# Turns at the shared port, a longer lead for the x blocks' loads, and another place for one block of sums

## The chip, the cores and the metric

One core of one Trainium2 chip. TensorE (PE) multiplies; VectorE (DVE), ScalarE (ACT) and GpSimd (POOL) do the elementwise work; SyncE (SP) issues most of the DMAs. The metric is the device time of one execution in microseconds, the median of three runs. Smaller is better.

## The reference

A chunked attention with memory tokens feeds a mixture of eight experts, all of which are computed for every token and summed with weights that a Sinkhorn iteration makes from the gate's logits. The attention's output `x` has 3072 rows and 512 columns.

```python
# attention: chunks of 32 queries see 16 keys to the left, 8 to the right, and 8 memory keys
out[:, :, c_start:c_end] = softmax(scale * q_c @ k_full.T) @ v_full
x = attn_out.transpose(0, 2, 1, 3).reshape(3072, 512)
# experts
P = sinkhorn(exp(x @ w_gate), 8 rounds)
for e in range(8):
    h = np.maximum(x @ w1[e], 0.0)        # 512 -> 1024
    out += P[:, e:e+1] * (h @ w2[e])      # 1024 -> 512
```

## The kernel before

**Units.** The experts' work is cut into 48 units of 512 tokens: six units for each of eight experts, numbered n = 0 to 47. Each float32 operand is held as two float16 parts (high and rest), and each product is three passes. The matrix products are done as Strassen-like products of blocks, seven instead of eight, so that each operand also has sums and differences of blocks, which VectorE and GpSimd make. From n = 14 (`DEEP`) on the first product has a second level of such blocks (`inner`, L2511 on PE, L2545 on ACT, L2556 on DVE).

**A unit's steps.** `paired` makes two of the four hidden blocks at a time: PE products into the PSUM tiles px, py, pz (L2607); ACT reads the first of a tile (L2637), DVE adds the next to it (L2647), and the results stand in `c_all` or `cs_late`. One more block, the relu of the last product, is written by ACT (L2727) into a block of ring `r` (L2722) and read by DVE's sums (L2740), which go to `ss_all`. Then ACT casts to the high parts (L2761, L2770), and the rest is taken as a difference: by DVE for the plain blocks (L2779), and for the sums (L2797) by GpSimd for one block of each pair and by DVE for the other. `output` multiplies the hidden blocks with w2 (yx, yy, yz, L2448) while the next unit's `paired` runs, in an order that a string gives (`WOVEN`): f is a step of the first pair, b of the second, x and y are steps of the two output blocks of the unit before, t makes an x block (below), i and j are the steps of `inner`. The results are scaled into `acc` and added to DRAM by GpSimd's accumulating DMA (L3199).

**Other work in the stretch from 344 us to 800 us.** The x blocks that the second level needs are made in `inner_x`, by tokens in n = 6 to 17: where they can't be read in place, two loads (L2143) bring the parts of x into slots of ring `pre`, a part of the tile `p_all`; DVE adds them (L2182), GpSimd takes four differences (L2199), ACT and DVE split the result (L2206, L2210), and it is stored (L2221). `scaled` uses the same ring `pre`: it loads sums of the first expert (L2931), ACT scales them (L2940), and they are stored again (L2950). The next expert's weights are loaded (L1322), combined by GpSimd (L1370, L1038), split by ACT (L840) and DVE (L849) and stored (L999, L1355). The second level's weight blocks come back by L1250; those of the second pair lie in `p_all`, and the first of them, slot (1, 0), is where ring `r` has been. `hand_over` (for n = 14) gives the place over: the load waits on all who used the last block of `r`.

**The order of the work.** Each engine works off its list in order, and the lists are written by a planner (`Plan`) before the launch. It keeps a clock for each engine and a model of the DMA queue, picks the task that can start first (among several, the one that is due first; `due` works the due times back from PE's), and emits its instructions. From about 300 us on it holds one of {DVE, GpSimd} back while the other holds an operation marked `port` (two inputs in SBUF), by at least `held - LOCK`. Nothing in the program enforces that order between the two engines when they run: only data dependences do. For a consumer of a load it adds a guard of 1.0 us (`GUARDS`) to the landing that it expects.

Two places of the emitted program matter below; DVE and GpSimd in the order in which the planner emitted them:

```
near 540 us: DVE L2779, POOL L1038, DVE L2647, DVE L2779, POOL L2797, DVE L849, POOL L1038, ..., DVE L2797, DVE L2647
near 953 us: DVE L2797, POOL L2662, DVE L849 (256), POOL L1370, POOL L2797, DVE L2647, DVE L849 (512), DVE L2647
```

Of the kernel before, what the change touches and what calls it, by code (L numbers as in the profile page):

```python
# [51 lines left out]
GUARDS = {"ACT": 1.0, "DVE": 1.0, "POOL": 1.0, "SP": 1.2, "PE": 0.0}  # L52
YIELDS = 0.7
PRESSED = 1.0
AFTER = 300.0
# [6 lines left out]
PACED = 1  # L62
EARLIER = 20.0
BESIDES = 0.8


class Task:


    __slots__ = ("eng", "cost", "fn", "prio", "left", "ready", "end", "then", "takes", "frees", "n", "dma", "start", "size", "port", "also", "first", "lead", "tag")  # L70

    def engines(self):
        return (self.eng,) if self.also is None else (self.eng, self.also[0])
# [56 lines left out]
class Plan:  # L130
# [8 lines left out]
    def __init__(self):  # L139
        self.tasks = []  # L140
        self.free = {}
        self.fill = None
        self.pipe = 0.0
        self.counted, self.asks, self.fetches = 0, ASKS, []
        self.held = {"DVE": 0.0, "POOL": 0.0}
        self.drift = 0.0
        self.late = 1 << 30

    def add(self, eng, cost, fn, deps=(), prio=0.0, bufs=(), takes=None, frees=None, dma=0.0,
            size=0, port=None, since=0.0, also=None, first=False, lead=0.0, tag=None):  # L150
        t = Task()
        t.tag = tag
        t.eng, t.cost, t.fn, t.prio, t.takes, t.frees = eng, cost, fn, prio, takes, frees
        t.ready, t.end, t.then, t.n, t.dma = since, None, [], len(self.tasks), dma
        t.size, t.also, t.first, t.lead = size, also, first, lead
        t.port = eng == "POOL" if port is None else port
        if dma:
            t.cost = cost * ISSUE
        before = {id(d): d for d in deps if d is not None}
        for b in bufs:  # L160
            assert not b.closed
            before.update(
                {id(d): d for d in b.before if tag is None or d.tag is None or d.tag == tag}
            )
            b.users.append(t)
        t.left = len(before)
        for d in before.values():
            d.then.append(t)
        if frees is not None:
            frees.left += 1  # L170
        self.tasks.append(t)
        return t
# [90 lines left out]
    def due(self):  # L263

        when = {}
        for t in reversed(self.tasks[self.late :]):
            if t.eng == "PE":
                when[id(t)] = t.prio
                continue
            by = [when[id(s)] for s in t.then if id(s) in when]  # L270
            if not by:
                continue
            lag = LANDS + READY + QUEUES + t.dma if t.dma else LAG + 0.15
            late = t.lead + (BESIDES if t.eng == "POOL" else 0.0)
            when[id(t)] = min(by) - lag - late - t.cost * (1.0 + SHARED / 2 if t.port else 1.0)
            if t.frees is not None:
                when[id(t)] = min(when[id(t)], t.prio + 200.0 + HOLD)
            if t.eng in ("ACT", "DVE", "POOL", "SP"):
                t.prio = when[id(t)]

    def run(self):
        self.due()
# [9 lines left out]
        while left:  # L292
# [71 lines left out]
            else:  # L364
                clock[t.eng] = t.end = at + t.cost
                if self.fill is not None and t.eng in ("ACT", "DVE"):
                    clock[t.eng] -= OVERLAP
            t.fn()
            if t.frees is not None:
                b = t.frees  # L370
                b.left -= 1
                b.end = max(b.end, t.end + 0.15)
                if b.left == 0:
                    heappush(self.free[b.group], (b.end, b.bank))
# [3 lines left out]
            for s in t.then:  # L378
                s.left -= 1
                late = lag  # L380
# [5 lines left out]

                    late = MARGIN if s.prio - t.end > FAR else RISK if t.end > 10.0 else 0.0
                elif t.dma and sure:
                    late = GUARDS.get(s.eng, 0.0)
                s.ready = max(s.ready, t.end + late)  # L390
                if s.left == 0:
                    for e in s.engines():
# [5 lines left out]
def tile_chunked_attn_sinkhorn_moe(  # L398
# [123 lines left out]
    akeep = [dram.tile([P, DM], F32, name=f"akeep_{T}") for T in range(NT)]  # L522

    plan = Plan()
    add = plan.add
    plan.free["main"] = [(0.0, 2)]
    plan.free["early"] = [(0.0, 7)]
# [1601 lines left out]
    def inner_x(u, at, op, again, inside):  # L2129
# [46 lines left out]
        def part(i):  # L2176
# [7 lines left out]
            at,  # L2184
            [*xs, st],
            port=True,
        )
        last = [t]
        for i, a, b in (
# [398 lines left out]
    def paired(e, u, which, hs, place="h"):  # L2588
# [112 lines left out]
        else:  # L2701
# [17 lines left out]
            c12 = plus(pz, at(1), at(1), [t3, r6], [c], pz)  # L2719
            yield  # L2720
            t4 = run(px, P4, True, [c22])
            m = rings["r"].take(lambda _: shaped(home("p", 0, 2), [P, 2, GT]))  # L2722
            rest = lambda: m.t
            r = add(
                "ACT",
# [817 lines left out]
    def given(which, side):  # L3543
# [8 lines left out]

    WOVEN = {
        "plain": "tfffffxyfxyffftxybxybtxybxybtxybbxybbxy",
        "thirds": "ijijijijijijijFxyFxytFxyFFxyFxyBxyBtxyBxyBBxyxy",
        "deep": "ijijijijijijijFxyFxyFxyFFxyBxyBxyBxyBxyxy",
        "end": "ijijijijijijijFxByFxByFxByFFWBBxyxyxyxyxyxy",
# [20 lines left out]
    def weave(n, front, pair, tokens):  # L3578
# [10 lines left out]
        then = pair(1, "w1") if end else pair(1)  # L3589
        inside = [inner(e, u, p) for p in range(2)] if deep else [None] * 2  # L3590
        lists = {"f": front, "b": then, "F": front, "B": then, "x": back[0:1], "y": back[1:2], "i": inside[0:1], "j": inside[1:2]}
        kind = "end" if end else "plain" if not deep else "thirds" if e == FINE else "deep"
        for ch in WOVEN[kind]:
            if ch == "t":
                if tokens:
# [23 lines left out]
        if n == DEEP - 1:  # L3619
            for k in range(3):  # L3620
                rings["wid"].after((0, k), rings["xs"].last[0].users)
            rings["xs"].last[0].closed = True
            rings["m"].after(0, [t for k in (2, 3) for t in rings["stage"].last[k].users])
            old = xops[units[n - 1][1]][0].users
            for pos in range(3):
                rings["xf"].after(pos, old)
# [29 lines left out]
    for n, (e, u) in enumerate(units):  # L3656
# [75 lines left out]
        if n == NU:  # L3732
# [10 lines left out]
            rings["sd"].after(0, users["s", 0] + users["s", 1])  # L3743
            rings["r"].after(0, users["p", 0] + users["p", 1])
        if n == FINE * NU - 1:
            ring_ = rings["stage"]
            ring_.order = [i for i in ((ring_.n + j) % 4 for j in range(4)) if i < 2]
            ring_.n = 0
# [88 lines left out]
```

## Time and profile before

| | before |
|---|---|
| median of 3 runs | 1906.11 us (1903.03 to 1908.89) |
| the profiled execution, its own time | 1909.26 us |
| its span, first to last instruction | 1907.5 us |
| PE busy | 1865.1 us (98%) |
| DVE / ACT / POOL busy | 1525.2 / 1063.0 / 914.5 us |
| mean granted TensorE clock | 0.994 |

The profiled execution's time is its span and 1.8 us around it; it lies 3.2 us above the median of the runs. Differences are worked out on the profiled execution's own span and then taken from the median.

### The profile page before, as it was taken

The page shows a single profiled execution, that of the slowest core. Times are in us where ns is not written, and L with a number is a line of the kernel's source. Part 1 is how long each engine was busy: PE and PEld are TensorE (multiplying, and loading weights), DVE is VectorE, ACT ScalarE, POOL GpSimd, SP SyncE. Part 2 cuts the span into 40 slices and gives each one's busy share as a digit, 9 for nine tenths or more (in the row PEclk, how much of TensorE's full clock was granted, in tenths as well). Part 3 has the DMA queues.
Part 4 walks back from the last instruction along what each step waited for, and adds up shares of the span by engine and source line. Part 5 has one row for each costly group of instructions (what it writes and reads, how often), then busy time and mean ns, then how long its engine had stood idle before and what let it go on. Part 6 is the DMA issues. An engine that isn't in the chain of part 4 may idle for free.

```text
span 1907.5 us, 52507 instructions
## 1 busy us (share of the span) xinstructions
PE 1865.1 (98%) x21788; PEld 1624.9 (85%) x21788; DVE 1525.2 (80%) x2203; ACT 1063.0 (56%) x1804; POOL 914.5 (48%) x950
## 2 busy tenths in 40 slices
PE   9999999999999899999999999999999999999999
PEld 5677666787888898889989998998989998999998
DVE  5887778787888577787888888887988878887774
ACT  6665454665665455555655655655556555554453
POOL 3541221635785365644555355553665355553233
PEclk9999999999999999999999999999999999999999
DMA  9968843288779856987768965898678976786453
GB/s 218 222 141 210 210 128 132 98 277 208 242 209 281 230 144 169 278 264 212 184 193 265 285 173 167 248 278 219 160 206 259 297 165 183 237 237 188 123 128 95
DMA packets 336491, 389.27 MB, mean 204 GB/s; under 512 B 122300, under 2 KB 226492, under 8 KB 334652
## 3 DMA queue, kind: packets, MB, share of 16 engines
q1 hardware_dynamic: 312636, 342.92, 58.5%
q0 software_dynamic: 23616, 43.00, 15.2%
q8 instruction: 170, 2.79, 0.6%
q14 instruction: 69, 0.57, 0.1%
HBM read 253.18 MB, written 137.89 MB: 205 GB/s over the span
## 4 chain that ended last, share of the span: by engine, by line
PE 88%; DVE 3%; DMA 3%; ACT 2%; issue 2%; SPq 0%; POOL 0%; DVEq 0%; POOLq 0%; ACTq 0%
PE yx L2448 21%; PE px L2607 18%; PE yz L2448 11%; PE yy L2448 6%; PE yp L3333 5%; PE ix_1i L2511 4%; PE ix_0i L2511 4%; PE px L2448 2%; PE iz_1i L2511 2%; PE iz_0i L2511 2%; PE pz L2607 2%; PE pz L2448 1%; PE iy_1i L2511 1%; PE iy_0i L2511 1%; PE yp L3396 1%
## 5 line engine op out<-in xcount | busy, mean ns | idle before, releaser
L2448 PEld LDWEIGHTS <-h_all 128*128 128x128 f16 x4704 | 461.8, 98 | 55.3 <-DVE h_all L2779 0.2
L2607 PEld LDWEIGHTS <-w_all 128*128 128x128 f16 x3888 | 380.1, 98 | 63.4 <-issue 18.6
L2448 PE MATMUL yx<-w_all,h_all 128*128 128x256 f16 x2592 | 325.6, 273 | 0.0
L2607 PE MATMUL px<-x_whole,w_all 128*128 128x256 f16 x2544 | 313.6, 273 | 11.9 <-DVE cs_late L2647 9.9
L2448 PEld LDWEIGHTS <-h_late 128*128 128x128 f16 x2268 | 221.8, 98 | 27.4 <-DVE h_late L2797 1.7
L3199 POOL DMA_DIRECT2D akeep<-acc x164 | 147.4, 979 | 127.6 <-ACT acc L3139 54.3
L2797 POOL TENSOR_TENSOR h_all<-ss_all,h_all 128x1024 f16<-128x1024 f32 x56 | 126.1, 2251 | 145.8 <-ACT h_all L2770 126.9
L3029 ACT ACTIVATE acc<-yx,pscale 128x256 f32<-128x256 f32 x164 | 77.3, 472 | 193.0 <-PE yx L2448 185.2
L2448 PE MATMUL yx<-w_all,h_late 128*128 128x256 f16 x1248 | 163.7, 273 | 1.4 <-DVE h_late L2797 1.4
L2448 PE MATMUL yz<-w_all,h_all 128*128 128x256 f16 x1296 | 165.0, 273 | 0.0
L2647 DVE SCALAR_TENSOR_TENSOR cs_late<-px,stage_high 128x512 f32<-128x512 f32 x102 | 70.4, 690 | 87.7 <-PE px L2607 69.4
L2511 PEld LDWEIGHTS <-w_all 128*128 128x128 f16 x2376 | 136.9, 98 | 2.4 <-DMA w_all<-wkeep 1.6
L1038 POOL TENSOR_TENSOR w2f<-w2f 128x256 f32<-128x256 f32 x88 | 94.6, 1075 | 74.4 <-DVE wp L849 69.9
L2770 ACT CAST h_all<-ss_all 128x1024 f16<-128x1024 f32 x112 | 114.1, 1039 | 27.5 <-DVE ss_all L2740 27.5
L2545 ACT ACTIVATE stage_high<-ix_0i 128x512 f32<-128x512 f32 (+1 forms) x102 | 59.6, 585 | 101.3 <-PE ix_0i L2511 99.9
L1038 POOL TENSOR_TENSOR w1b<-w1b 128x256 f32<-128x256 f32 x88 | 94.2, 1071 | 38.2 <-DVE wp L849 27.1
L2797 POOL TENSOR_TENSOR h_late<-ss_all,h_late 128x1024 f16<-128x1024 f32 x27 | 59.7, 2211 | 91.6 <-ACT h_late L2770 86.5
L2607 PE MATMUL px<-x,w_all 128*128 128x256 f16 x768 | 95.4, 275 | 5.2 <-ACT cs_late L2637 4.4
L2448 PEld LDWEIGHTS <-w_all 128*128 128x128 f16 x924 | 89.2, 98 | 13.1 <-issue 1.4
L3333 PE MATMUL yp<-w_all,h_all 128*128 128x512 f16 x432 | 100.0, 379 | 0.0
L2647 DVE SCALAR_TENSOR_TENSOR c_all<-px,x_whole 128x512 f32<-128x512 f32 x102 | 70.1, 687 | 31.9 <-PE px L2607 31.0
L2662 POOL TENSOR_TENSOR stage_high<-stage_high 128x512 f32<-128x512 f32 x34 | 50.8, 1495 | 89.5 <-ACT stage_high L2545 68.3
(347 smaller groups left out, 4244.9 us busy)
## 6 DMA issues: line engine op xcount, KB each, us to landing
x_whole<-xkeep SPq DMA_DIRECT2D x203, 256.0 KB
akeep<-acc POOLq DMA_DIRECT2D x164, 256.0 KB, 5.6
wkeep<-wp SPq DMA_DIRECT2D x48, 512.0 KB
w_all<-wkeep SPq DMA_DIRECT2D x84, 256.0 KB
w_all<-wkeep SPq DMA_DIRECT2D x42, 512.0 KB
wkeep<-wp SPq DMA_DIRECT2D x48, 384.0 KB
wx_late<-ikeep SPq DMA_DIRECT2D x58, 256.0 KB
more<-ikeep SPq DMA_DIRECT2D x55, 256.0 KB
```

What stands on the lines that cost most here:

```text
L1038: lambda d=d, p=p, q=q, op=op: nc.gpsimd.tensor_tensor(d(), p(), q(), op=op),
L2448: nc.tensor.matmul(dst.t, a, b, start=(not more and n == 0), stop=(n == end), skip_group_check=more,)
L2511: nc.tensor.matmul(dst.t[:, k], left(k, op[0], wl), right(k, op[1], xl), start=(not more and n == 0 and k == 0), stop=(n == 2), skip_group ...
L2545: lambda: nc.scalar.activation(at(*to), src.t, AF.Copy, scale=DOWN),
L2607: nc.tensor.matmul(dst.t[:, f], ws[f][1](wl, kt), part(xl, kt), start=(not more and f == 0 and n == 0), stop=(n == 5), skip_group_check=True,)
L2647: lambda: nc.vector.scalar_tensor_tensor(to(), src.t, DOWN, other(), op0=ALU.mult, op1=ALU.add),
L2662: lambda: nc.gpsimd.tensor_tensor(part(2)(), part(2)(), part(1)(), op=ALU.add),
L2770: lambda f=f, h=h: nc.scalar.copy(h.t[:, 0, 3:7], s.t[:, f]),
L2797: lambda f=f, h=h, eng=nc.gpsimd if aside else nc.vector: eng.tensor_tensor(h.t[:, 1, 3:7], s.t[:, f], h.t[:, 0, 3:7], op=ALU.subtract),
L3029: lambda: nc.scalar.activation(acc.t[:, cols], src.t, AF.Copy, scale=f),
L3199: lambda a=a, dst=dst: nc.gpsimd.dma_start(dst, a.t, accum_op=ALU.add),
L3333: nc.tensor.matmul(py.t, hf.t[:, hl, where[fh], o : o + P], room(fp, WIDE * wl + DM * fh, WIDE * wl + DM * (fh + 1)), start=(fp == 0 and i ...
```

## The change

Four edits. (1) `turn`: from 300 us on, after a DVE task marked `port` is emitted, its last instruction is remembered; the next `port` task of GpSimd gets a wait on it. Each remembered instruction is used once: the first GpSimd operation after it waits, those that follow have only GpSimd's own order. GpSimd's DMA issues get no such wait, and nothing makes DVE wait on GpSimd. In the program before, the rule would give 262 GpSimd instructions a wait after 300 us. (2) `WARY`: where x parts are loaded for `inner_x`, the loads (L2143) are due 3 us earlier, and the planner lets the DVE add (L2182) start 3 us later after the landing that it expects. (3) The block of ring `r` that the second pair of n = 13 uses lies in `stage_high` in place of `p_all`; the load of slot (1, 0) then waits on the block of the first pair, and ring `m`, whose first block is `stage_high`, waits on the new one. (4) Unit n = 12 has an order of its own: the first pair's seven products all run ahead of the first x and y.

```diff
--- before.py
+++ after.py
@@ -62,12 +62,13 @@
 PACED = 1
 EARLIER = 20.0
 BESIDES = 0.8
+WARY = 3.0
 
 
 class Task:
 
 
-    __slots__ = ("eng", "cost", "fn", "prio", "left", "ready", "end", "then", "takes", "frees", "n", "dma", "start", "size", "port", "also", "first", "lead", "tag")
+    __slots__ = ("eng", "cost", "fn", "prio", "left", "ready", "end", "then", "takes", "frees", "n", "dma", "start", "size", "port", "also", "first", "lead", "tag", "wary")
 
     def engines(self):
         return (self.eng,) if self.also is None else (self.eng, self.also[0])
@@ -145,11 +146,12 @@
         self.held = {"DVE": 0.0, "POOL": 0.0}
         self.drift = 0.0
         self.late = 1 << 30
+        self.front = None
 
     def add(self, eng, cost, fn, deps=(), prio=0.0, bufs=(), takes=None, frees=None, dma=0.0,
-            size=0, port=None, since=0.0, also=None, first=False, lead=0.0, tag=None):
+            size=0, port=None, since=0.0, also=None, first=False, lead=0.0, tag=None, wary=0.0):
         t = Task()
-        t.tag = tag
+        t.tag, t.wary = tag, wary
         t.eng, t.cost, t.fn, t.prio, t.takes, t.frees = eng, cost, fn, prio, takes, frees
         t.ready, t.end, t.then, t.n, t.dma = since, None, [], len(self.tasks), dma
         t.size, t.also, t.first, t.lead = size, also, first, lead
@@ -267,7 +269,7 @@
             if t.eng == "PE":
                 when[id(t)] = t.prio
                 continue
-            by = [when[id(s)] for s in t.then if id(s) in when]
+            by = [when[id(s)] - (s.wary if t.dma else 0.0) for s in t.then if id(s) in when]
             if not by:
                 continue
             lag = LANDS + READY + QUEUES + t.dma if t.dma else LAG + 0.15
@@ -277,6 +279,21 @@
                 when[id(t)] = min(when[id(t)], t.prio + 200.0 + HOLD)
             if t.eng in ("ACT", "DVE", "POOL", "SP"):
                 t.prio = when[id(t)]
+
+    def turn(self, t):
+
+        eng = {"DVE": mybir.EngineType.DVE, "POOL": mybir.EngineType.Pool}[t.eng]
+        inst = next(i for i in reversed(self.tc.nc.cur_bb.bb.instructions) if i.engine == eng)
+        if t.eng == "DVE":
+            self.front = inst.name
+        elif self.front is not None:
+            self.tc.add_manual_dep(
+                inst,
+                self.front,
+                mybir.DependencyInfo(mybir.DependencyClass.Sync, mybir.DependencyReason.DATA),
+                reason="turns at the port",
+            )
+            self.front = None
 
     def run(self):
         self.due()
@@ -366,6 +383,8 @@
                 if self.fill is not None and t.eng in ("ACT", "DVE"):
                     clock[t.eng] -= OVERLAP
             t.fn()
+            if self.fill is None and at > AFTER and t.port and not t.dma:
+                self.turn(t)
             if t.frees is not None:
                 b = t.frees
                 b.left -= 1
@@ -386,7 +405,7 @@
 
                     late = MARGIN if s.prio - t.end > FAR else RISK if t.end > 10.0 else 0.0
                 elif t.dma and sure:
-                    late = GUARDS.get(s.eng, 0.0)
+                    late = GUARDS.get(s.eng, 0.0) + s.wary
                 s.ready = max(s.ready, t.end + late)
                 if s.left == 0:
                     for e in s.engines():
@@ -522,6 +541,7 @@
     akeep = [dram.tile([P, DM], F32, name=f"akeep_{T}") for T in range(NT)]
 
     plan = Plan()
+    plan.tc = tc
     add = plan.add
     plan.free["main"] = [(0.0, 2)]
     plan.free["early"] = [(0.0, 7)]
@@ -2184,6 +2204,7 @@
             at,
             [*xs, st],
             port=True,
+            wary=WARY if again else 0.0,
         )
         last = [t]
         for i, a, b in (
@@ -2719,7 +2740,10 @@
             c12 = plus(pz, at(1), at(1), [t3, r6], [c], pz)
             yield
             t4 = run(px, P4, True, [c22])
-            m = rings["r"].take(lambda _: shaped(home("p", 0, 2), [P, 2, GT]))
+            m = rings["r"].take(
+                lambda k: shaped(high[:, 0 : 2 * GT] if k else home("p", 0, 2), [P, 2, GT]),
+                int(which == 1 and (e, u) == units[DEEP - 1]),
+            )
             rest = lambda: m.t
             r = add(
                 "ACT",
@@ -3552,6 +3576,7 @@
 
     WOVEN = {
         "plain": "tfffffxyfxyffftxybxybtxybxybtxybbxybbxy",
+        "opens": "tfffffffxyfxyftxybxybtxybxybtxybbxybbxy",
         "thirds": "ijijijijijijijFxyFxytFxyFFxyFxyBxyBtxyBxyBBxyxy",
         "deep": "ijijijijijijijFxyFxyFxyFFxyBxyBxyBxyBxyxy",
         "end": "ijijijijijijijFxByFxByFxByFFWBBxyxyxyxyxyxy",
@@ -3589,7 +3614,7 @@
         then = pair(1, "w1") if end else pair(1)
         inside = [inner(e, u, p) for p in range(2)] if deep else [None] * 2
         lists = {"f": front, "b": then, "F": front, "B": then, "x": back[0:1], "y": back[1:2], "i": inside[0:1], "j": inside[1:2]}
-        kind = "end" if end else "plain" if not deep else "thirds" if e == FINE else "deep"
+        kind = "end" if end else "thirds" if deep and e == FINE else "deep" if deep else "opens" if n == FINE * NU else "plain"
         for ch in WOVEN[kind]:
             if ch == "t":
                 if tokens:
@@ -3620,7 +3645,8 @@
             for k in range(3):
                 rings["wid"].after((0, k), rings["xs"].last[0].users)
             rings["xs"].last[0].closed = True
-            rings["m"].after(0, [t for k in (2, 3) for t in rings["stage"].last[k].users])
+            rings["m"].after(0, rings["r"].last[1].users)
+            rings["r"].last[1].closed = True
             old = xops[units[n - 1][1]][0].users
             for pos in range(3):
                 rings["xf"].after(pos, old)
@@ -3743,6 +3769,7 @@
             rings["sd"].after(0, users["s", 0] + users["s", 1])
             rings["r"].after(0, users["p", 0] + users["p", 1])
         if n == FINE * NU - 1:
+            rings["r"].after(1, [t for k in (2, 3) for t in rings["stage"].last[k].users])
             ring_ = rings["stage"]
             ring_.order = [i for i in ((ring_.n + j) % 4 for j in range(4)) if i < 2]
             ring_.n = 0
```

## Rows read from the trace of the kernel before

**Rows 1.** The page's part 1: busy time and share of PE.
```profile
PE 1865.1 (98%) x21788; PEld 1624.9 (85%) x21788; DVE 1525.2 (80%) x2203; ACT 1063.0 (56%) x1804; POOL 914.5 (48%) x950
```
**Rows 2.** PE's waits: line, releaser, us in total, times, longest.
```profile
PE px L2607 <- DVE cs_late L2647: 10.6, 6, 2.4
PE iz_1i L2511 <- DMA p_all<-wikeep: 5.0, 1, 5.0
```
**Rows 3.** Busy time by stretch: PE, PEld, DVE, ACT, POOL, clock, DMA, GB/s.
```profile
640.00:660.00 20.00, 15.00 (x186) 14.19 (x185) 8.47 (x14) 8.59 (x15) 6.36 (x6) 0.91 0.81 170
```
**Rows 4.** PE's timeline, second level of n = 14 and of n = 16.
```profile
651.93 0.80 PE L2511 MATMUL iz_1i<-wx_late,p_all 128*128 128x128 f16 x6 [5.00 <-DMA p_all<-wikeep]
...
658.95 1.47 PE L2607 MATMUL px<-x_whole,w_all 128*128 128x256 f16 x12
...
725.13 0.50 PE L2511 MATMUL iz_1i<-wx_late,p_all 128*128 128x128 f16 x6
...
726.18 0.49 PE L2511 MATMUL ix_0i<-wx_late 128*128 128x128 f16 x6 [0.38 <-ACT stage_high L2545]
...
731.20 1.47 PE L2607 MATMUL px<-x_whole,w_all 128*128 128x256 f16 x12
```
**Rows 5.** Timelines of DVE, ACT and SP's queue around 645 us.
```profile
627.79 0.68 DVE L2740 SCALAR_TENSOR_TENSOR ss_all<-cs_late,p_all 128x512 f32<-128x512 f32 x1
...
643.51 1.29 DVE L2740 SCALAR_TENSOR_TENSOR ss_all<-c_all,p_all 128x512 f32<-128x512 f32 x2 [1.50 <-ACT p_all L2727]
...
648.74 0.49 ACT L2545 ACTIVATE x_whole<-ix_1i 128x384 f32<-128x384 f32 x1
...
644.87 0.34 SPq L1250 DMA_DIRECT2D p_all<-wikeep  x1
```
**Rows 6.** Timelines around 458 us: PE, ACT, DVE, SP's queue.
```profile
461.93 2.72 PE L2607 MATMUL px<-x,w_all 128*128 128x256 f16 x12 [4.41 <-ACT cs_late L2637]
...
460.15 0.51 ACT L2940 ACTIVATE p_all<-p_all,pscale 128x256 f32<-128x256 f32 x1 [5.93 <-DMA p_all<-akeep]
...
456.56 0.69 DVE L2182 TENSOR_TENSOR wx_late<-p_all 128x512 f32<-128x512 f16 x1 [4.47 <-DMA p_all<-xkeep]
...
450.08 0.47 SPq L2143 DMA_DIRECT2D p_all<-xkeep  x1
450.60 3.38 SPq L1322 DMA_DIRECT2D stage_high<-in_moe_w_dram  x4
...
454.67 6.00 SPq L2931 DMA_DIRECT2D p_all<-akeep  x3
```
**Rows 7.** Timelines of DVE, POOL and PE around 540 us.
```profile
536.45 0.94 DVE L2779 SCALAR_TENSOR_TENSOR h_all<-c_all,h_all 128x768 f16<-128x768 f32 x1
...
537.92 2.98 DVE L2779 SCALAR_TENSOR_TENSOR h_all<-c_all,h_all 128x768 f16<-128x768 f32 x1
...
536.54 3.50 POOL L2797 TENSOR_TENSOR h_all<-ss_all,h_all 128x1024 f16<-128x1024 f32 x1
...
544.08 1.47 PE L2607 MATMUL px<-x,w_all 128*128 128x256 f16 x12 [0.74 <-DVE cs_late L2647]
```
**Rows 8.** Timelines of DVE, POOL and PE around 955 us.
```profile
953.51 4.98 DVE L849 SCALAR_TENSOR_TENSOR wp<-w1b,sw,wp 128x512 f16<-128x512 f32 x1
...
953.90 1.55 POOL L2662 TENSOR_TENSOR stage_high<-stage_high 128x512 f32<-128x512 f32 x1
...
955.54 2.40 POOL L2797 TENSOR_TENSOR h_all<-ss_all,h_all 128x1024 f16<-128x1024 f32 x1
...
959.14 2.72 PE L2607 MATMUL px<-x_whole,w_all 128*128 128x256 f16 x12 [2.41 <-DVE cs_late L2647]
```
**Rows 9.** Timelines of POOL, DVE and PE in n = 12.
```profile
585.75 2.13 POOL L2797 TENSOR_TENSOR h_late<-ss_all,h_late 128x1024 f16<-128x1024 f32 x1 [5.14 <-DVE acc L3071]
...
589.50 1.22 DVE L2797 TENSOR_TENSOR h_late<-ss_all,h_late 128x1024 f16<-128x1024 f32 x1
...
590.77 0.94 PE L2448 MATMUL yx<-w_all,h_late 128*128 128x256 f16 x7 [1.45 <-DVE h_late L2797]
```

## The prediction, made before the result was known

> **What bounds the kernel now.** I read the page's part 1 first: TensorE is busy for 98% of the span [rows 1], so no other engine's busy time is worth anything in itself. All that a change in the order of work can give back are TensorE's holes, 1907.5 - 1865.1 = 42 us, and what a lower clock costs behind some of them. Edits 1 to 4 act only from about 300 us on (the planner's late part), so the holes of the attention stretch ahead of it stay.
>
> Second, the table of TensorE's waits says who ends the holes [rows 2], and the timelines say when. From 344 us on there are few long ones: 4.4 us at 457 [rows 6], 0.7 at 543 [rows 7], 1.45 at 589 [rows 9], 5.0 at 647 [rows 4], and four of 2.4 at 956, 1176, 1394 and 1610, which are one pattern, once for each of four experts [rows 8]; the group shows the first, and they are four of the six waits in the first row of the table [rows 2]. The rest are 1.4 us or less each. Third, for each hole, I read the timelines of the engine that ended it, to see what stood in front of the late instruction in that engine's list.
>
> The clock: in the stretch from 640 to 660 the granted clock is 0.91 [rows 3], so part of it ran at the lower level, 1.2 GHz instead of 2.4, behind the hole of 5.0. What that cost: from iz_1i to px there are the same products in n = 14 and in n = 16, 658.95 - 651.93 = 7.02 against 731.20 - 725.13 = 6.07, of which 0.38 is a hole [rows 4]. So 7.02 - 5.69 = 1.3 us are the clock's.
>
> **Edit 3, the place of one block of sums.** The hole of 5.0 ends with the landing of the load of slot (1, 0) [rows 4]. SP issued it at 644.87, just when VectorE's last two readers of ring `r`'s block, 643.51 to 644.80, were done [rows 5]; it landed 7 us later. With the block of the second pair in `stage_high`, the load waits on the readers of the first pair's block. These end at 628.5 [rows 5], so it can go 16 us earlier and is in place some 11 us before TensorE asks for it at 646.9. The cost of what is added: the relu is written and read as before, in another tile; the inner block's first write to `stage_high` now waits for the same two VectorE sums. It is wanted when TensorE comes back to that tile, 0.67 us after iz_1i's start in n = 16 [rows 4], at 647.6; a write takes 0.49 [rows 5] and the sums end at 644.80, so over 2 us of cover are left by the inner level's first four products; if the sums came later by more than that, their lateness would appear in the hole of ix_0i.
>
> What is late next: ScalarE writes x_whole<-ix_1i only at 648.74 to 649.23 [rows 5], behind casts for h_all that were put ahead of it. Without the DMA's hole, TensorE comes to the product that needs it about 1.2 us after iz_1i's start (as 725.13 to 726.18 less 0.38, and the next product of 0.5 [rows 4]), so at about 648.1. If ScalarE keeps that order, a hole of 1.2 opens; if the planner, which no longer expects a late load, puts the short read first, there is none. The nearest row is the same place in n = 16, 0.38 [rows 4]; I take 0.4, with 0 to 1.2 as bounds. Edit 3: 5.0 + 1.3 - 0.4 = 5.9 us (5.1 to 6.3).
>
> **Edit 1, turns at the port.** Near 540 us GpSimd's L2797 starts at 536.54, VectorE's second L2779 at 537.92, and this takes 2.98 where the one ahead of it took 0.94 [rows 7]. In the emitted order that L2779 stands directly ahead of GpSimd's L2797, so the turn falls on the right instruction: GpSimd would start behind it. VectorE gains up to 2 us, and TensorE's hole of 0.74, which ended with a VectorE instruction queued behind, goes. I take 0.7; bounds 0 and 0.74. What GpSimd then does later is its L2797 by some 2 us, and behind it two differences and DMA issues for data of the next expert; its h block is used after the plain blocks' products, so nothing on TensorE waits on it here.
>
> At 955 us it is otherwise. VectorE's L849 takes 4.98 while GpSimd runs L2662, L1370 and L2797 without a break [rows 8]; this holds up c12 and makes the hole of 2.4. But in the emitted order GpSimd's L1370 and L2797 stand ahead of this L849. Their turns are taken by the VectorE instructions before it, long over: GpSimd is behind the plan here, and the edit has no wait in the other direction. So I count nothing for these four holes; the other bound, that all go, is 4 x 2.4 = 9.6 us and the clock's part, 2.72 - 1.47 = 1.25 for this one [rows 7, 8], say 12 in all.
>
> One rule speaks against edit 1. The trace first: VectorE's L849 started at 953.51 and was not through when L2662 ended at 955.45, but only after L2797, 957.94 [rows 8]: it was passed over between two GpSimd instructions. The Trainium skill ("SBUF — State Buffer", Who interferes with whom) calls the port pair an exclusive lock, held for one instruction by whichever engine issues first. By that rule the turn only moves the same block from VectorE to GpSimd, edit 1 would be worth 0 and the sum below 6.6; by the trace, which disagrees in that a late VectorE instruction pays for several GpSimd instructions, it is worth 0.7.
>
> **Edit 4, the order in n = 12.** The hole of 1.45 at 589 ends with VectorE's L2797 at 589.50 [rows 9]. In the new string that product still has the same seven f, two b and the earlier x and y in front of it, so TensorE comes to it no later; what can change is the lists of VectorE and ScalarE, since the first pair's sums are ready earlier. Bounds 0 and 1.45; I take half, 0.7. No instruction is added.
>
> **Edit 2, the lead.** VectorE's add L2182 waits 4.47 us at 452 to 456.5 for its load [rows 6]; the edit puts other work in front of it. But the hole at 457 doesn't come from there. It ends with ScalarE's L2637, which is queued behind L2940; and that waits 5.93 for a load of `scaled`, issued by SP at 454.67, behind four weight loads of 3.38 [rows 6]. That load gets no lead. Its bounds: if the new order of SP's queue happens to put it in front of the weight loads, 4.4 + 1.3 of clock = 5.7 us go; if the led x loads take its place in the queue instead, it is later by one issue, 0.47 [rows 6], and the hole grows by that. I count 0, the nearer row.
>
> **The sum.** 5.9 + 0.7 + 0.7 + 0 = 7.3 us off the span of 1907.5, to 1900.2. The profiled execution's own time, 1909.26, is 3.2 above the median; I take the difference from the median: 1906.1 - 7.3 = 1898.8 us. This kernel's measurement tells a difference of some 0.3%, 5.7 us, from none; the forecast is just beyond.
>
> **Rivals.**
> - *SP's new order clears the hole at 457 too.* For: edit 2 moves the due times in that queue, at that place. Against: not of the load that is late. 7.3 + 5.7 = 13.0: 1893.1 us.
> - *The four starved L849 are cured as well*, because the new plan puts them ahead of GpSimd's run. For: the planner's list is remade. Against: the pattern came out the same for four experts with different starts. 7.3 + 12 = 19.3: 1886.8 us.
> - *The load's hole is replaced.* ScalarE's order stays (hole 1.2), the clock still falls behind it or the sums come late into `stage_high`, and edits 1 and 4 move nothing: 5.0 - 1.2 = 3.8, and 1.3 of clock kept: 1902.3 us, no change that can be told.
> - *A new hole like that of 457 elsewhere*, since all loads between 344 and 640 are ordered anew while the DMA queue is full: 7.3 - 5.7 = 1.6: 1904.5 us.
> - *Slower: the turn holds GpSimd's h block.* In n = 7 to 12 GpSimd's L2797 can be close to its use: 585.75 to 587.88, with TensorE at that product at 589 [rows 9]. Were it given its turn behind VectorE's L2797, 589.50 to 590.72, it would end at 592.9: a hole of some 3.9 and 1.3 of clock, 5.2 us. Three such units of the six cost 15.6 against 7.3: 1914.4 us; it decides from the third. Against: in the present list it stands ahead of that instruction.
>
> **Chances.** Forecast 0.48, with its own range 1894 to 1902; first rival 0.17; second 0.07; third 0.11; fourth 0.09; slower 0.08. Faster by over 0.3% means under 1900.4: three quarters of the forecast's 0.48, and the first two rivals, 0.60. Slower: the last rival and a little of the fourth, 0.10. Within: 0.30. Leaving out the second and the last rival (0.15), the range runs from 1888 to 1908.
>
> **What the profile after would show.** Edit 3: p_all<-wikeep issued well before 640, no wait of iz_1i on a DMA, at most 1.2 us on ScalarE's x_whole, clock 1.00 from 640 to 660. Edit 1: VectorE's L2779 near 540 back at 0.95, GpSimd's L2797 behind it; at 955, 1176, 1394 and 1610 L849 still at about 5 us and the hole still 2.4. Edit 2: L2182 no longer waiting, the ScalarE wait at 457 still there. The prediction is wrong if those four holes are gone, if ScalarE's wait on L2931 is gone, or if TensorE waits on h_all or h_late at places where it did not.

## The result, and the profile after

The changed kernel takes 1878.36 us (median; 1877.90 to 1879.52) beside 1904.57 (1902.98 to 1908.89) for the kernel before in the same job: a ratio of 0.986, 95% interval 0.9841 to 0.9878. The gain is 0.014 x 1904.6 = 26.7 us where 7.3 were forecast, and the time lies below the range. The profiled execution has a span of 1877.5 us against 1907.5, 30.0 less.

In the changed kernel's file the lines stand about 20 lower down: L849 is L869, L1038 L1058, L1370 L1390, L2607 L2628, L2637 L2658, L2647 L2668, L2779 L2803, L2797 L2821, L2931 L2955, L2940 L2964. Kernels of the experiments differ from that by up to 2.

Part 1 of the page of the changed kernel, which answers to [rows 1]:

```profile
PE 1855.1 (99%) x21788; PEld 1619.5 (86%) x21788; DVE 1486.8 (79%) x2203; ACT 1064.1 (57%) x1804; POOL 865.4 (46%) x950
```

TensorE's idle time went from 42.4 us to 1877.5 - 1855.1 = 22.4. The other 10.0 us are busy time with the same 21788 matmuls: the mean granted clock rose from 0.994 to 1.000, and 0.6% of 1865 is 11. So two thirds of these 30.0 us are holes and one third is the clock. Not all of the clock is the edits' work: before, the granted clock was 0.83 from 20 to 40 us, ahead of anything that they touch, beside 460 to 480 (0.83), 640 to 660 (0.91), 940 to 980 (0.97 and 0.94) and 1600 to 1620 (0.91), which stand behind holes that went.

But for n = 12, TensorE's matmuls come in the same order in both kernels, so one and the same matmul can be looked up in both profiled executions. By its start, the changed kernel is 1.0 us ahead at 343 us, before any edit shows. It gains 7.2 us across the hole at 457, 0.9 across that at 543, 1.6 at 589, 6.7 at 647, and 4.0, 2.5, 2.5 and 4.1 at the four of [rows 8]: 29.5 in all; what is gained and lost elsewhere comes to half a us.

VectorE and GpSimd lost 38.4 and 49.1 us of busy time with the same instruction counts; more on that at the end.

The table of TensorE's waits in the changed kernel, for [rows 2] (line, releaser, us in total, times, longest):

```profile
PE ix_1i L2532 <- ACT x_whole L2566: 3.3, 5, 1.4
...
PE px L2628 <- DVE c_all L2668: 1.0, 1, 1.0
...
PE px L2628 <- DVE cs_late L2668: 0.8, 1, 0.8
```

The row of 10.6 us for VectorE's cs_late is down to 0.8, the 5.0 us on the DMA are gone, and there is no row left for ScalarE's cs_late, which made the hole at 457. Now the places, in timelines of the changed kernel. The second level of n = 14, for [rows 4, 5], and then the window that answers to [rows 3]:

```profile
637.10 0.50 PE L2532 MATMUL iz_1i<-wx_late,p_all 128*128 128x128 f16 x6
...
642.62 1.47 PE L2628 MATMUL px<-x_whole,w_all 128*128 128x256 f16 x12
...
619.42 0.32 SPq L1270 DMA_DIRECT2D p_all<-wikeep  x1
...
633.80 1.29 DVE L2764 SCALAR_TENSOR_TENSOR ss_all<-c_all,stage_high 128x512 f32<-128x512 f32 x2 [1.45 <-ACT stage_high L2751]
...
636.34 0.49 ACT L2566 ACTIVATE stage_high<-ix_0i 128x384 f32<-128x384 f32 x1
636.79 0.49 ACT L2566 ACTIVATE x_whole<-ix_1i 128x384 f32<-128x384 f32 x1
```

```profile
640.00:660.00 20.00, 20.00 (x210) 18.20 (x208) 17.31 (x29) 11.36 (x20) 9.73 (x12) 1.00 0.59 177
```

The load is issued 17.7 us before TensorE's use of it, where it was 7.1. VectorE's sums are through with `stage_high` at 635.1 and the inner block's first write there starts at 636.34. From iz_1i to px it is 5.52 us, where it was 7.02, and the clock is 1.00.

Around 458 us, for [rows 6], SP's queue and ScalarE:

```profile
447.37 0.47 SPq L2163 DMA_DIRECT2D p_all<-xkeep  x1
447.89 2.25 SPq L1342 DMA_DIRECT2D stage_high<-in_moe_w_dram  x4
450.24 0.52 SPq L2974 DMA_DIRECT2D akeep<-p_all  x1
450.86 0.43 SPq L2955 DMA_DIRECT2D p_all<-akeep  x1
...
455.37 0.51 ACT L2964 ACTIVATE p_all<-p_all,pscale 128x256 f32<-128x256 f32 x1 [1.07 <-DMA p_all<-akeep]
```

The whole train of x load, four weight loads and load of `scaled` runs some 3 us earlier: the x load at 447.37 (before 450.08), the late load at 450.86 (454.67). ScalarE waits 1.07 for it instead of 5.93, and TensorE not at all.

At the first of the four starved L849, three more lines of the kernel before beside [rows 8], and then VectorE and GpSimd in the changed kernel:

```profile
953.48 0.75 POOL L1370 TENSOR_TENSOR ws_halves<-w1b,w1b 128x128 f32<-128x128 f32 x1
...
955.12 0.73 POOL L1370 TENSOR_TENSOR ws_halves<-w1b,ws_halves 128x128 f32<-128x128 f32 x1
...
959.02 0.73 DVE L849 SCALAR_TENSOR_TENSOR ws_halves<-ws_halves,sw 128x512 f16<-128x512 f32 x1
```

```profile
937.83 2.51 DVE L869 SCALAR_TENSOR_TENSOR wp<-w1b,sw,wp 128x512 f16<-128x512 f32 x1
940.26 0.68 DVE L2668 SCALAR_TENSOR_TENSOR cs_late<-px,stage_high 128x512 f32<-128x512 f32 x1
941.73 1.84 DVE L869 SCALAR_TENSOR_TENSOR ws_halves<-ws_halves,sw 128x512 f16<-128x512 f32 x1 [0.79 <-ACT ws_halves L860]
...
936.10 0.55 POOL L1390 TENSOR_TENSOR ws_halves<-w1b 128x128 f32<-128x128 f32 x1 [9.30 <-DMA wikeep<-ws_halves]
...
937.80 0.75 POOL L1390 TENSOR_TENSOR ws_halves<-w1b,w1b 128x128 f32<-128x128 f32 x1
938.22 1.56 POOL L2683 TENSOR_TENSOR stage_high<-stage_high 128x512 f32<-128x512 f32 x1
940.48 0.46 POOL L1390 TENSOR_TENSOR ws_halves<-w1b,ws_halves 128x128 f32<-128x128 f32 x1 [0.70 <-DVE wp L869]
940.89 2.13 POOL L2821 TENSOR_TENSOR h_all<-ss_all,h_all 128x1024 f16<-128x1024 f32 x1
```

The bracket at 940.48 is the turn: the last of the four L1390 waits on L869. In both kernels the third of them starts 0.03 us ahead of VectorE's instruction, and L2683 (L2662 before) after it. Before, the fourth and L2797 followed without a break, and L849 ended 0.55 us behind L2797; now L869 ends 0.56 behind L2683. It takes 2.51 instead of 4.98, and c12, the VectorE instruction behind it, comes in time. The next L869 takes 1.84 where it took 0.73, with L2821 beside it, and TensorE doesn't wait for that. GpSimd's h block ends 5.2 us after L869's start where it ended 4.4 after it, and nothing waits for it.

### The profile page after: what moved, and what is told of

It reads as the page before. It is cut to its first block, busy times and chain, and to the rows that moved or that the text cites. A ratio compares the mean times of both kernels' runs of the same rounds, so it can differ in the third digit from the quotient of the medians.

```text
span 1877.5 us, 52657 instructions
## 1 busy us (share of the span) xinstructions
PE 1855.1 (99%) x21788; PEld 1619.5 (86%) x21788; DVE 1486.8 (79%) x2203; ACT 1064.1 (57%) x1804; POOL 865.4 (46%) x950
## 4 chain that ended last, share of the span: by engine, by line
PE 92%; DMA 3%; DVE 2%; ACT 1%; issue 1%; SPq 1%; POOL 0%; DVEq 0%; POOLq 0%; ACTq 0%
PE yx L2469 23%; PE px L2628 19%; PE yz L2469 11%; PE yy L2469 6%; PE yp L3357 5%; PE ix_1i L2532 4%; PE ix_0i L2532 4%; PE px L2469 2%; PE pz L2628 2%; PE iz_0i L2532 2%; PE iz_1i L2532 2%; PE pz L2469 1%; PE iy_0i L2532 1%; PE iy_1i L2532 1%; PE yp L3420 1%; PE py L2628 1%
## 5 line engine op out<-in xcount | busy, mean ns | idle before, releaser
L2628 PEld LDWEIGHTS <-w_all 128*128 128x128 f16 x3888 | 379.0, 98 | 46.2 <-issue 2.3
L2628 PE MATMUL px<-x_whole,w_all 128*128 128x256 f16 x2544 | 312.4, 273 | 1.8 <-DVE c_all L2668 1.0
L2821 POOL TENSOR_TENSOR h_all<-ss_all,h_all 128x1024 f16<-128x1024 f32 x56 | 122.8, 2192 | 124.5 <-ACT h_all L2794 49.3
L2668 DVE SCALAR_TENSOR_TENSOR cs_late<-px,stage_high 128x512 f32<-128x512 f32 x102 | 70.4, 690 | 91.4 <-PE px L2628 70.4
L1058 POOL TENSOR_TENSOR w2f<-w2f 128x256 f32<-128x256 f32 x88 | 77.8, 884 | 83.8 <-DVE wp L869 32.5
L1058 POOL TENSOR_TENSOR w1b<-w1b 128x256 f32<-128x256 f32 x88 | 79.9, 909 | 48.8 <-issue 9.4
L2821 POOL TENSOR_TENSOR h_late<-ss_all,h_late 128x1024 f16<-128x1024 f32 x27 | 57.6, 2134 | 81.2 <-ACT h_late L2794 45.3
L2628 PE MATMUL px<-x,w_all 128*128 128x256 f16 x768 | 94.1, 273 | 0.0
L2668 DVE SCALAR_TENSOR_TENSOR c_all<-px,x_whole 128x512 f32<-128x512 f32 x102 | 70.2, 688 | 24.3 <-PE px L2628 22.9
L2821 DVE TENSOR_TENSOR h_all<-ss_all,h_all 128x1024 f16<-128x1024 f32 x56 | 81.8, 1460 | 5.6 <-ACT h_all L2794 5.6
```

Of the source, the lines that this page charges most:

```text
L1058: lambda d=d, p=p, q=q, op=op: nc.gpsimd.tensor_tensor(d(), p(), q(), op=op),
L2628: nc.tensor.matmul(dst.t[:, f], ws[f][1](wl, kt), part(xl, kt), start=(not more and f == 0 and n == 0), stop=(n == 5), skip_group_check=True,)
L2668: lambda: nc.vector.scalar_tensor_tensor(to(), src.t, DOWN, other(), op0=ALU.mult, op1=ALU.add),
L2821: lambda f=f, h=h, eng=nc.gpsimd if aside else nc.vector: eng.tensor_tensor(h.t[:, 1, 3:7], s.t[:, f], h.t[:, 0, 3:7], op=ALU.subtract),
```

## The experiments

The ratios are to the kernel before on the same chip; 1% is 19 us.

| kernel | ratio | 95% interval |
|---|---|---|
| edit 1 alone | 0.9934 | 0.9910 to 0.9958 |
| edit 2 alone | 0.9960 | 0.9943 to 0.9977 |
| edit 3 alone | 0.9981 | 0.9964 to 0.9998 |
| edit 4 alone | 0.9994 | 0.9978 to 1.0010 |
| all but edit 1 | 0.9950 | 0.9933 to 0.9968 |
| all but edit 2 | 0.9901 | 0.9873 to 0.9930 |
| all but edit 3 | 0.9906 | 0.9876 to 0.9936 |
| all but edit 4 | 0.9874 | 0.9842 to 0.9906 |
| edit 1, waits behind L849 only | 0.9919 | 0.9904 to 0.9934 |
| edit 1, all other waits | 0.9971 | 0.9949 to 0.9993 |
| edit 2, earlier due only | 0.9942 | 0.9925 to 0.9958 |
| edit 2, later add only | 0.9997 | 0.9978 to 1.0016 |
| all edits, waits behind L849 only | 0.9861 | 0.9836 to 0.9886 |
| all edits, again | 0.9858 | 0.9832 to 0.9884 |

One kernel "without" an edit is the changed kernel with that edit undone as the diff shows; "alone" has the other three undone.

**Edit 1, the turns.** Undone by

```diff
-            if self.fill is None and at > AFTER and t.port and not t.dma:
-                self.turn(t)
```

Alone:

> Edit 1 alone on the kernel before. Theory T (the turn itself cures the four starved L849, because in the planner's order GpSimd's fourth L1370 comes behind L849, not ahead of it): the four holes of 2.4 us near 956, 1176, 1394 and 1610 and what the clock costs behind two of them go, and the 0.7 near 543: some 12 to 14 us less than before, L849 (512 columns) near 954 at about 2.5 us in place of 4.98. The holes of 4.4 at 457 and 5.0 at 647 stay. Rival P (the four went because edits 2 to 4 made the planner's list anew, as on record in the prediction): 0.7 us less at most, L849 still at 4.98.

All but it:

> The changed kernel without edit 1. If the turn alone cures the four starved L849: the four holes of 2.4 come back with the clock behind some of them, 1878 + 10 to 13 = 1888 to 1891 us. If the remade list had a part in it, less comes back.

Alone 0.66%, 12.6 us; taken out of the whole, 0.90%. TensorE's waits with edit 1 alone, and with all but edit 1:

```profile
PE iz_1i L2532 <- DMA p_all<-wikeep: 5.3, 1, 5.3
PE px L2628 <- ACT cs_late L2658: 4.8, 2, 4.6
```

```profile
PE px L2626 <- DVE cs_late L2666: 12.3, 7, 2.4
```

With the turns alone, the holes at 457 and 647 stay and VectorE's cs_late is off the head of the table; without them it leads the table, and the holes of 457 and 647 are gone. The plan of "edit 1 alone" is that of the kernel before, instruction for instruction, so no remade list did this: the wait did. With it the four starved L869 (512 columns) take 2.50 to 2.51 us, where they took 4.98 to 4.99.

The hole of 0.7 near 543 is gone too, but not by the turn behind L2779 (here L2803) that the prediction names. GpSimd there, with edit 1 alone:

```profile
541.60 0.72 POOL L1058 TENSOR_TENSOR stage_high<-stage_high 128x256 f32<-128x256 f32 x1 [1.24 <-DVE h_all L2821]
542.30 2.11 POOL L2821 TENSOR_TENSOR h_all<-ss_all,h_all 128x1024 f16<-128x1024 f32 x1
```

In the planner's order GpSimd's h block stands behind an L1058 whose turn falls on VectorE's own h block.

Then the waits themselves were divided, in the plan of the kernel before. A flag marks the VectorE tasks that `split` adds (L849), and the wait is given only behind those, or (`not self.half`) only behind the others:

```diff
-            self.front = inst.name
+            self.front, self.half = inst.name, t.half
...
-            self.tc.add_manual_dep(
+            if self.half:
+                self.tc.add_manual_dep(
```

Only behind L849:

> Edit 1 alone, and of its waits only those that stand behind VectorE's L849 (101 of 384 in the planner's order); the plan is that of the kernel before. Theory: the four holes of 2.4 us near 956, 1176, 1394 and 1610 hang on one such wait for each expert, L1370 behind L849; all four go, the small hole near 543, which hangs on a turn behind L2779, stays; ratio 0.994 to 0.996, nearly all of the 0.9934 that edit 1 gave alone. Rival: the gain is spread over many waits; then about a quarter of it, 0.998, is here.

Only behind the others:

> Edit 1 alone, and of its waits all but those behind VectorE's L849 (283 of 384); the plan is that of the kernel before. Theory: the four holes of 2.4 us stay, the one near 543 goes; ratio 0.998 to 1.0. Rival, the gain is spread: three quarters of it are here, 0.995.

GpSimd with the waits behind L849 only; then VectorE, GpSimd and TensorE with the others only:

```profile
949.97 1.55 POOL L2685 TENSOR_TENSOR stage_high<-stage_high 128x512 f32<-128x512 f32 x1
952.22 0.46 POOL L1392 TENSOR_TENSOR ws_halves<-w1b,ws_halves 128x128 f32<-128x128 f32 x1 [0.70 <-DVE wp L870]
```

```profile
954.38 4.98 DVE L870 SCALAR_TENSOR_TENSOR wp<-w1b,sw,wp 128x512 f16<-128x512 f32 x1
...
954.77 1.55 POOL L2685 TENSOR_TENSOR stage_high<-stage_high 128x512 f32<-128x512 f32 x1
955.99 0.73 POOL L1392 TENSOR_TENSOR ws_halves<-w1b,ws_halves 128x128 f32<-128x128 f32 x1
956.40 2.39 POOL L2823 TENSOR_TENSOR h_all<-ss_all,h_all 128x1024 f16<-128x1024 f32 x1
...
960.01 1.47 PE L2630 MATMUL px<-x_whole,w_all 128*128 128x256 f16 x12 [2.41 <-DVE cs_late L2670]
```

The quarter of the waits that stands behind L849 (101 of 384) carries all of edit 1 (0.81%, the whole 0.66%, intervals overlapping). That of these only one for each expert matters was not tried. The small hole near 543 was expected to stay and is down to 0.2. With the others the first place is as it was before, 4.98 and 2.41; in that profile three of the four holes are there, and the hole of 0.7 near 543 is gone. Their 0.29% lies between the two expectations, so what they are worth in the kernel before stays open between 1 and 10 us. In the changed kernel it was tried directly:

> The changed kernel with, of its waits, only those behind VectorE's L849. Theory: these carry the whole worth of edit 1, the other three quarters only take busy time from VectorE and GpSimd that nothing waits for; ratio equal to that of the changed kernel in the same job, within 0.3%, holes of 2.4 us absent. Rival: the other waits hold GpSimd up for nothing; then this kernel is faster than the changed one by some 0.1 to 0.2% (edit 1 alone gave 0.9934, with these waits alone 0.9919). Second rival: in the changed plan the others are worth something, 0.3% as by the runs with all but these waits; then it is slower by that.

> The changed kernel as it is, beside the one with the waits behind L849 alone, on the same chip: ratio 0.984 to 0.988.

0.9861 and 0.9858: what the other three quarters of the waits are worth or cost there can't be told from nothing. Neither rival shows; what the intervals leave to either is a quarter of a per cent.

**Edit 2, the lead.** Undone by

```diff
-WARY = 3.0
+WARY = 0.0
```

Alone:

> Edit 2 alone. Theory W (the lead changes the order of SP's queue so that ScalarE's load of scaled is no longer behind two groups of weight loads): the hole of 4.4 near 457 goes with the lower clock behind it, 6 to 7 us less. Rival (on record): the hole stays, 0 us. Under rival P the four holes of 2.4 could go here too: 18 us less.

All but it:

> The changed kernel without edit 2. If the lead is what cures the hole at 457: 4.4 to 5.9 us of hole on ScalarE's cs_late come back with 1 to 3 of clock, 1884 to 1887 us. If the other edits cure it too, 1878 us.

Alone 0.40%, 7.6 us, and the hole at 457 is gone. Not all of the gain is that hole's: the hole at 589 is gone with it too, and edit 3's is 1.9 in place of 5.0. Without edit 2 the hole at 457 is back, at the head of TensorE's waits in that kernel, where the same matmul loses 6.7 us across it. TensorE's waits with edit 2 alone, and with all but it:

```profile
PE iz_1i L2530 <- DMA p_all<-wikeep: 1.9, 1, 1.9
```

```profile
PE px L2628 <- ACT cs_late L2658: 3.7, 1, 3.7
```

Its two halves, on the kernel before. The earlier due time only, and the later add only:

```diff
-                    late = GUARDS.get(s.eng, 0.0) + s.wary
+                    late = GUARDS.get(s.eng, 0.0)
```

```diff
-            by = [when[id(s)] - (s.wary if t.dma else 0.0) for s in t.then if id(s) in when]
+            by = [when[id(s)] for s in t.then if id(s) in when]
```

> Edit 2 alone, and of it only the half that makes the loads L2143 due 3 us earlier; the planner's guard for the adds behind them stays at 1.0 us. Theory: the hole near 457 hangs on the place of scaled's load in SP's queue, which the earlier due times shift; it goes, ratio 0.996 to 0.997 as edit 2 alone gave. Rival: it hangs on the add being planned later, so that DVE and ACT do other work first; then the hole of 4 to 6 us stays, ratio 1.0.

> Edit 2 alone, and of it only the half that lets the planner put the add L2182 3 us later behind its load; the loads' due times are those of the kernel before. Theory: SP's queue keeps the order of the kernel before up to that place, so the hole near 457 stays, 4 to 6 us, and the ratio is 0.999 to 1.001. Rival: it goes, ratio 0.996 to 0.997.

SP's queue, ScalarE and TensorE, first with the due half, then with the add half:

```profile
448.03 2.22 SPq L1340 DMA_DIRECT2D stage_high<-in_moe_w_dram  x4
450.91 0.43 SPq L2953 DMA_DIRECT2D p_all<-akeep  x1
...
457.31 0.51 ACT L2962 ACTIVATE p_all<-p_all,pscale 128x256 f32<-128x256 f32 x1 [3.23 <-DMA p_all<-akeep]
...
460.03 2.08 PE L2626 MATMUL px<-x,w_all 128*128 128x256 f16 x12 [2.65 <-ACT cs_late L2656]
```

```profile
448.82 2.34 SPq L1340 DMA_DIRECT2D stage_high<-in_moe_w_dram  x4
452.48 8.30 SPq L2953 DMA_DIRECT2D p_all<-akeep  x2
...
463.51 1.87 PE L2626 MATMUL px<-x,w_all 128*128 128x256 f16 x8 [8.70 <-ACT cs_late L2656]
```

The earlier due time moves the load of `scaled` to 450.91, as in the changed kernel, and carries the whole gain (0.58%); the later add alone is worth nothing and its hole is larger. But the due half leaves 2.65 of the hole, where "gone" was expected: issued at the same time, the load lets ScalarE begin 6.4 us later here and 4.5 later in the changed kernel. Part of the 0.58% is also one of the four holes of 2.4, which is absent in that profile. Nor does an earlier issue clear the hole by itself. SP's queue and ScalarE with all but edit 2:

```profile
450.17 7.72 SPq L2955 DMA_DIRECT2D p_all<-akeep  x3
...
457.23 0.51 ACT L2964 ACTIVATE p_all<-p_all,pscale 128x256 f32<-128x256 f32 x1 [5.19 <-DMA p_all<-akeep]
```

There the load leaves 5.2 us before TensorE wants the result (2.9 in the kernel before, 6.6 in the changed one), but ScalarE begins 7.1 us behind the issue, and the hole is 3.7. From this kernel to the changed one the earlier issue is worth 1.4 us and the quicker landing 2.5; from the kernel before they are 3.7 and 1.0. What makes that landing quicker or slower stays open.

**Edit 3, the place.** Undone by

```diff
-                int(which == 1 and (e, u) == units[DEEP - 1]),
+                0,
...
-            rings["m"].after(0, rings["r"].last[1].users)
-            rings["r"].last[1].closed = True
+            rings["m"].after(0, [t for k in (2, 3) for t in rings["stage"].last[k].users])
```

Alone:

> Edit 3 alone. The load of slot (1, 0) is issued some 16 us earlier, the hole of 5.0 at 647 goes, and with it 1.3 us of lower clock; a wait on ScalarE's x_whole of 0 to 1.2 is left: 5 to 6.3 us less. Rival P: the four holes of 2.4 go as well, 17 us less.

All but it:

> The changed kernel without edit 3. With edit 2 alone the hole of iz_1i on its load was 1.9 and not 5.0, without the lower clock behind it. If that holds here, 1.9 us come back: 1880 us. If the load's lateness is its own, 5 to 6.3: 1883 to 1885 us.

Alone it gave 0.19%, 3.6 us (0.4 to 6.9); taken out of the whole it costs 0.46%, 8.8 us. TensorE's waits with it alone, and with all but it:

```profile
PE px L2626 <- DVE cs_late L2666: 12.8, 7, 2.4
PE px L2626 <- ACT cs_late L2656: 5.9, 1, 5.9
```

```profile
PE iz_1i L2532 <- DMA p_all<-wikeep: 5.6, 1, 5.6
```

Alone it clears the hole of the load and the remade plan gives part back: 5.9 instead of 4.4 at 457, and 12.8 instead of 10.6 on VectorE's cs_late. By the same matmul's start it gains 5.8 us across that hole, and loses 1.7 at 457 and 3.0 between 720 and 780. With the other edits there, nothing is given back: against all but edit 3, the changed kernel gains 7.4 at this place. The hole of 1.9 that edit 2 alone leaves there did not carry over: without edit 3 it is 5.6.

**Edit 4, the order in n = 12.** Undone by

```diff
-        kind = "end" if end else "thirds" if deep and e == FINE else "deep" if deep else "opens" if n == FINE * NU else "plain"
+        kind = "end" if end else "thirds" if deep and e == FINE else "deep" if deep else "plain"
```

Alone:

> Edit 4 alone. The hole of 1.45 near 589 goes or stays: 0 to 1.5 us less, which can't be told from no change by the time; the profile decides. Rival P: the four holes go, 12 us less.

All but it:

> The changed kernel without edit 4. With edit 2 alone the hole at 589 was gone already, so nothing comes back: 1878 us. If edit 4 is needed for it beside the others: 1.5 us more, 1880 us.

Alone 0.06%, with an interval over zero; taken out, 0.14%, with overlapping intervals. Alone it clears the hole of 1.45 at 589 and a hole of 3.5 opens near 1330, in a unit that it doesn't touch:

```profile
1332.76 2.50 PE L2626 MATMUL px<-x_whole,w_all 128*128 128x256 f16 x11 [3.51 <-DVE c_all L2666]
```

The hole at 589 is absent without edit 4 too, and with edit 2 alone; it was not edit 4's to give in the whole.

## Why the prediction was wrong, point by point

**Edit 1: the step that failed.** It reads: "But in the emitted order GpSimd's L1370 and L2797 stand ahead of this L849. Their turns are taken by the VectorE instructions before it, long over." That order, and the list in the front section, were read from the compiled program's list of instructions. That is not the planner's order, in which `turn` acts: there L849 with 512 columns stands ahead of the fourth L1370 and of L2797, as the bracket at 952.22 shows in the plan of the kernel before, and that at 940.48 in the new one. Also the count of 262 waits comes from that list; by the planner's order it is 384. So the four holes, counted 0 with "the other bound" 12, went: 12.6 us measured alone, and 13.1 by the four places in the changed kernel. The size of the bound was right; the choice between the bounds hung on an order that had not been established. "GpSimd is behind the plan here" was right, and is why the wait pays: after 9.3 us on a DMA, GpSimd would run its backlog ahead of a VectorE instruction that the plan had put first. The second rival had this place and price, but its way, a remade list, was wrong: edit 1 alone keeps the old one. The small hole at 543 went, as forecast, but by another wait than the one named, which came from the same list; that is luck.

**The rule weighed there.** In this trace, with the turns one GpSimd instruction that starts after L869 passes it, and it takes 2.51; with no turn at that place three do, and it takes 4.98. The wait took 2.5 us of standing off an instruction on which TensorE waits; GpSimd's h block comes 0.8 us later and VectorE's next L869 takes 1.1 longer, with TensorE waiting for neither. Once for each of four experts, that is the four holes. By the Trainium skill ("SBUF — State Buffer", Who interferes with whom), whichever of the two engines issues first has the port pair for its whole instruction, and the prediction drew from it that edit 1 is worth 0. That the standing moves agrees with the trace; that a move is worth nothing doesn't follow. Which engine goes next, the trace shows: the third L1390 started at 937.80, L869 at 937.83 and L2683 at 938.22, and L869 ends 0.6 us behind L2683.

**Edit 2: counted 0, worth 7.6 us alone.** "That load gets no lead" is true, and the conclusion was not. A due time can move whatever stands in the same queue; the train in front of the late load left some 3 us earlier, the load 3.8, and it landed faster by 1 us (ScalarE begins 4.5 behind the issue, before 5.5). The first rival had the place; its way, the load put in front of the weight loads, was wrong: it still stands behind four of them. Its price, 5.7, was short of the 7.2 that the place gave: the hole of 4.4 was right, and the clock behind it cost 2.8, not 1.3.

**Edit 3: right in mechanism.** 5.9 us forecast, 3.6 alone and 8.8 in the whole, and the forecast is within what either can tell. The place gave 6.7 in the changed kernel. The load left early, the clock stayed at 1.00, and `stage_high` was free in time. The 0.4 us for ScalarE's x_whole didn't come: that write stands at 636.79, ahead of the casts.

**Edit 4: 0.7 forecast, 1.1 alone**, not to be told from nothing, and the hole went without it: edit 2 clears it too.

**The sum.** With the two terms at their other bounds the prediction's own sum is 7.3 + 12 + 5.7 = 25.0; measured were 26.7. By place, 13.1 stand beside the bound of 12, 7.2 beside 5.7, and 6.7 beside 5.9. So no price was far off; two choices were. That the four edits alone add up to 12.6 + 7.6 + 3.6 + 1.1 = 24.9 is partly chance: edit 2 alone takes from the holes of edits 3 and 4, and edit 3 alone gives part back. The two rivals that held them were each taken as happening alone, and the range had no room for both. Of the three signs that the prediction named against itself, the first appeared, the four holes gone, and the second nearly, ScalarE's wait on the load cut from 5.93 to 1.07. The third appeared as well, but small, one wait on h_all where there was none:

```profile
397.70 0.94 PE L2469 MATMUL yx<-w_all,h_all 128*128 128x256 f16 x7 [0.93 <-DVE h_all L2821]
```

It is on VectorE's block, and edit 2 alone has it too (0.69), so it isn't the turn holding up GpSimd's block, which the slower rival meant.

## What to carry to other kernels

Where a change acts on the order in which a planner emits, establish that order from the planner itself before an edit is priced at nothing by it; the list of a compiled program shows each engine's own order, not the order between engines. When one engine falls behind its plan behind a DMA, ask which neighbour its backlog will pass over when it comes free; the 101 waits behind that neighbour were worth as much as all 384. And when due times of one kind of load are moved, follow every load in that queue, its landing too: most of the gain was at a load that the edit doesn't name.

## What the runs showed of the hardware

A VectorE instruction with two inputs in SBUF, once it stands behind a GpSimd instruction, is passed over by GpSimd instructions that start after it and follow without a break: with three of them it took 4.98 us, with one 2.51, and one of the same size with nothing on GpSimd beside it 0.73 [rows 8 and the lines beside them].

Part of the recorded busy time of the two engines is such standing. Part 1 of the page with the waits other than behind L849, then with those behind L849 only, both in the plan of the kernel before:

```profile
PE 1863.6 (98%) x21788; PEld 1624.7 (85%) x21788; DVE 1483.2 (78%) x2203; ACT 1064.0 (56%) x1804; POOL 866.5 (45%) x950
```

```profile
PE 1858.5 (98%) x21788; PEld 1622.0 (86%) x21788; DVE 1501.4 (79%) x2203; ACT 1063.1 (56%) x1804; POOL 899.7 (48%) x950
```

Against [rows 1], the first takes 42.0 us off VectorE and 48.0 off GpSimd and saved 0.29%; the second takes 23.8 and 14.8 and saved 0.81%. The busy time saved says nothing of the time: what counts is for whom TensorE waits.
